# Spreading the output factors with VectorE's block transposes instead of a TensorE product

## The chip, the cores and the metric

The kernel runs on one core of a Trainium2 chip. The metric is the device time of one execution in microseconds. The core has five engines that run side by side and wait for each other through semaphores: TensorE (PE) multiplies matrices into PSUM, VectorE (DVE) and ScalarE (ACT) do elementwise work, GpSimd (POOL) does what is given to it of the same, SyncE (SP) issues most of the DMAs. Each engine runs its own instructions in the order in which the program gives them. ScalarE's queue can issue DMAs as well, and here it issues the few small ones at the start.

## The reference

Two stages follow each other. The first is causal attention with a decay in place of a softmax, over 8 batches, 8 heads, 576 positions and a head size of 64; the second is a feed-forward layer of 4608 tokens that takes the maximum of three products:

```python
scores = scale * np.matmul(q, k.transpose(0, 1, 3, 2))
gamma = 1.0 - 2.0 ** (-5.0 - np.arange(H, dtype=np.float32))
Dmat = np.where(rel >= 0, gamma[:, None, None] ** rel[None, :, :], 0.0)   # rel = query position - key position
x = np.matmul(scores * Dmat, v)            # then (B, H, S, D) -> (B*S, H*D)
h = np.maximum(np.maximum(x @ w1, x @ w2), x @ w3)
out = h @ w_out
```

The weights w1, w2, w3 and w_out come as 64-bit floats.

## The kernel before, in words

The tokens are cut into 36 chunks of 128 (`g`) and 9 tiles of 512 tokens (`t`). The decay gamma^(i-j) is split into a factor of the key, gamma^(-j), and one of the query, gamma^i / 8. The first is multiplied into v (`vd`, from `raws["v"]` and `gk`, line 273). The second, the output factor, is multiplied into the finished attention output when it goes from PSUM to SBUF (`xT`, line 224 through `output`, lines 550 to 559). It stands in `gq`, a tile of 128 partitions by 4 by 128: partition half c and index n belong to head 4c+n, the last axis is the position in the chunk, and all 64 partitions of a half hold the same numbers. A state carried from chunk to chunk (`state`, `keep`) brings in the older keys.

The order of all work is written out by hand: the framework's own ordering is off, and each engine gets its instructions in the order in which the Python code emits them. Lines 1060 to 1102 write the start, chunks 0 to 3. In that order:

- the memsets and the small DMAs: the rows of output factors (line 159) and the key factors `gk` (line 160), both on ScalarE's queue; ScalarE's table load and first copy follow (line 162);
- `warm(6)` (line 179), products of a tile of ones that only keep TensorE busy;
- `load(g)` (line 262): k, q and v of a chunk, 256 KB each, on SyncE's queue, with the first weights (`bits`, line 609) between them;
- `decay(0)`: vd of chunk 0, on GpSimd (line 273; also for chunks 1 and 2);
- `transposes(0)` (lines 298 and 299): TensorE transposes k (`kt`) and q (`qt`) of the chunk, ScalarE copies them out of PSUM as kT and qT;
- `scores(0)` (line 312), with VectorE's masks `st` (line 224 through `soon`), and `state(0)` (`kv`, line 425);
- `transposes(1)`, `decay(1)`;
- the product of the output factors (line 1082) and its copy from PSUM to `gq` (line 1083);
- `values(0)` (`o`, line 466), `keep(0)` (line 433), `scores(1)`, the factors multiplied into chunk 0's output (`xT`), `state(1)`, `transposes(2)`, `keep(1)`;
- `convert(2)`: the first two steps of turning 64-bit weights into 32-bit ones: `expo` (line 777) and `frac` (line 786) on VectorE with three operations of ScalarE (lines 779, 785 and 788); then `values(1)` and so on.

PSUM tiles come from pools with a fixed number of buffers that are handed out in turn. `ps_y` has two: the warming products, the product of the factors and the two `o` tiles of a chunk take turns in them. The second `o` tile of chunk 0 gets the buffer in which the factors were.

After the start the tiles of 512 tokens follow. In tile 0 the weights are converted by VectorE and ScalarE while TensorE does the plain products (`up`, line 934). From tile 1 on the feed-forward products are done by a scheme with fewer multiplications and more sums (line 909), with attention chunks between them.

How the factors reach `gq` before: two DMAs bring the 8 rows of 128 factors to two partitions, one for each half of the heads (`factors[0:2]`). `spreader[0:2, 1, :]` is a 2 by 128 matrix with ones where row c belongs to partition half c, made by a memset and two affine selects on GpSimd (lines 171 to 173). Their product is 128 partitions by 512, in one PSUM bank, with each factor row on all 64 partitions of its half; one copy takes it to `gq`.

Of the kernel before, what the change touches and what calls it, by code (L numbers as in the profile page):

```python
# [40 lines left out]
FP32 = mybir.dt.float32  # L41
# [4 lines left out]
ALU = mybir.AluOpType  # L46
PSUM = bass.MemoryType.PSUM

C = 128
# [49 lines left out]
def kernel(  # L99
# [14 lines left out]
    nc = tc.nc  # L114
    P = 128
    B, H, S, D = q.shape
    N, DM = out.shape
    DF = moe_w1.shape[1]
    NP = H // 2
# [12 lines left out]
    ppool = ctx.enter_context(tc.tile_pool(name="ppool", bufs=PARTS))  # L132
# [7 lines left out]
    ps_y = ctx.enter_context(tc.tile_pool(name="ps_y", bufs=2, space=PSUM))  # L140
# [4 lines left out]
    def half(j):  # L145
        return slice(D * j, D * (j + 1))
# [5 lines left out]
    const.tile([P, FILL // 4], FP32, name="fill")  # L152
    gq = const.tile([P, NP, C], FP32, name="gq")
    spreader = ppool.tile([P, NP, C], FP32, tag="part", name="spreader")
    for n in range(2):
        nc.vector.memset(spreader[:, n, :], 1.0)
    factors = ppool.tile([P, NP, C], FP32, tag="part", name="factors")
    for b in range(2):
        nc.scalar.dma_start(factors[0:2, b::2, :], out_decay[D * b].rearrange("(c u) x -> c u x", c=2))
    nc.scalar.dma_start(gk[:], key_decay)  # L160
    nc.vector.memset(one[:], 1.0)
    nc.scalar.copy(first[:], one[:])
# [4 lines left out]
    nc.gpsimd.memset(causal[:], 1.0)  # L167
    nc.gpsimd.affine_select(out=causal[:], in_=causal[:], compare_op=ALU.is_ge, fill=0.0,
                            base=0, channel_multiplier=-1, pattern=[[1, C]])

    for base, cm, step in ((0, -D, 1), (D - 1, D, -1)):
        nc.gpsimd.affine_select(out=spreader[0:2, 1, :], in_=spreader[0:2, 1, :], compare_op=ALU.is_ge, fill=0.0,
                                base=base, channel_multiplier=cm, pattern=[[step, P]])

    def warm(n):

        ps = ps_y.tile([P, P], FP32, tag="y", name="warm")
        for _ in range(n):
            nc.tensor.matmul(ps[:], lhsT=spreader[:, 0, :], rhs=spreader[:, 0, :], start=True, stop=True)
# [39 lines left out]
    def soon(step):  # L219

        if spread:
            urgent.append(step)
        else:
            step()
# [39 lines left out]
    def decay(g):  # L264
        factor = gk[:].unsqueeze(2).to_broadcast([C, H, D])
        t = raws.pop(("v", g))
        if spread or g >= CPT + 2:
            vds[g] = t
            scaling.extend(partial(nc.scalar.mul, t[:, h, :], t[:, h, :], gk[:, h:h + 1]) for h in range(H))
            return  # L270
        vds[g] = vpool.tile([C, H, D], FP32, tag="s", name="vd")
        engine = nc.gpsimd if g < CPT - 1 else nc.vector
        engine.tensor_tensor(vds[g][:], t[:], factor, op=ALU.mult)

    def pair(t, p):
        return t[:, 2 * p:2 * p + 2, :].rearrange("a h d -> a (h d)")

    def transposes(g, names="kq"):
        both = qks.setdefault(g, {})
        if both:  # L280
            pass
        elif g >= BY_CHUNKS:
            for n, tag in (("k", "kT"), ("q", "m1")):
                both[n] = att.tile([P, H, D], FP32, tag=tag, name=n + "T", bufs=2 if n == "k" else 3)
        else:
            both["k"] = att.tile([P, NP, C], FP32, tag="kT", name="kT", bufs=2)
            both["q"] = ppool.tile([P, NP, C], FP32, tag="part", name="qT")
        if g >= BY_PE:
            for n in ("k", "q"):
                soon(partial(nc.vector.transpose, both[n][:].rearrange("a p c -> a (p c)"),  # L290
                             raws.pop(("kx" if n == "k" else n, g))[:].rearrange("a x y i -> a (x y i)")))
            return
        for n in names:
            src = raws["k", g] if n == "k" else raws.pop(("q", g))
            pool, tag = (ps_r, "r") if g >= CPT else (ps_x, "x")
            pt = pool.tile([P, NP, C], FP32, tag=tag, name=n + "t")
            for p in range(NP):
                nc.tensor.transpose(pt[:, p, :], pair(src, p), ident[:C, :C])
            nc.scalar.copy(both[n][:], pt[:])
# [148 lines left out]
    def values(chunks, new_states=(), later=False, middle=()):  # L448

        def before(g):
            return C if start_of(g) is None else start_of(g)

        chore(len(urgent))
        t, i = divmod(chunks[0], CPT)
        if chunks[0] >= CPT:
            (chunk_values if chunks[0] >= BY_CHUNKS else parity_values)(chunks, t, i)
            return
        pool, tag = (ps_r, "r") if chunks[0] >= CPT - 1 else (ps_y, "y")  # L460
        o = [pool.tile([P, len(chunks), NP // 2, C], FP32, tag=tag, name="o") for _ in range(2)]
        for m, g in enumerate(chunks):
            for n in range(NP):
                for c in range(2):
                    h = head(c, n)
                    nc.tensor.matmul(o[n % 2][half(c), m, n // 2, :], lhsT=vds[g][:, h, :],
                                     rhs=sts[g, h % 2][:, h // 2, :], start=m == 0 and n < 2,
                                     stop=before(g) == 0, skip_group_check=True)
        for g in new_states:
            if g not in kvs:  # L470
                state(g)
        for step in middle:
            step()
        for m, g in enumerate(chunks):
            old = before(g)
            if old > 0:
                for n in range(NP):
                    for c in range(2):
                        h = head(c, n)
                        r = half(h % 2)  # L480
                        nc.tensor.matmul(o[n % 2][half(c), m, n // 2, :old], lhsT=states[g][r, h // 2, :],
                                         rhs=qks[g]["q"][r, h // 2, :old], start=False, stop=True,
                                         skip_group_check=True)
        finish = partial(output, chunks, o, t, i)
        if later:
            return finish
        finish()
# [582 lines left out]
    load_weights(2)  # L1070
    decay(0)

    transposes(0)
    warm(2)
    for j in range(2):
# [2 lines left out]
    state(0)  # L1078
    transposes(1)
    decay(1)  # L1080
    spread_factors = ps_y.tile([P, NP, C], FP32, tag="y", name="factors")
    nc.tensor.matmul(spread_factors[:], lhsT=spreader[0:2, 1, :], rhs=factors[0:2], start=True, stop=True)
    nc.vector.tensor_copy(gq[:], spread_factors[:])
    first_output = values([0], [0], later=True)
    keep(0)
    scores(1)
# [116 lines left out]
```

## Time and profile before

| | us |
|---|---|
| median of 3 runs (742.96 to 743.14) | 743.0 |
| the profiled execution, its own time | 742.99 |
| its span, first to last instruction | 740.9 |
| TensorE busy | 735.6 (99%) |
| VectorE busy | 575.2 (78%) |
| ScalarE busy | 344.7 (47%) |
| GpSimd busy | 37.2 (5%) |
| product of the factors, line 1082 (two records) | 0.59 and 0.69 |
| copy to `gq`, line 1083 | 0.69 |
| issue of the two factor DMAs on ScalarE's queue | 1.28 and 0.63 |

The profile is one execution. All times in it count from the first instruction. A matrix product of 32-bit floats shows as two records. L1082 is line 1082 of the kernel; operations that go through a helper are listed under the helper's line (224 for `soon`, 577 for sums), so that the names of the tiles tell them apart. An arrow in `vd<-vraw,gk` points from what is read to what is written. In lines with square brackets, the bracket holds the time that the engine stood idle before, and what ended it. Matmuls are pipelined, and a busy TensorE is not one at its peak.

### The profile page before, as it was taken

Reading aid. Unit: us, or ns where it says so; the run is one execution under the profiler, and the core shown is the slowest. Engines: PE = TensorE matmul, PEld = TensorE weight load, DVE = VectorE, ACT = ScalarE, POOL = GpSimd, SP = SyncE. Lnnn points to the kernel's source line nnn. Section 1 sums busy time; section 2 is a strip of 40 time slices with the busy share of each in tenths; the row PEclk is TensorE's granted clock in tenths of the full one; section 3 lists DMA queues with packets and bytes.
Section 4 is the critical chain, followed back from the end, with each engine's and each line's share of the span. In section 5 each row is a group of like instructions: output and inputs, shape, how many; then the busy total and the mean of one; then the engine's idle time right before and its main releaser. Section 6 shows DMA issues by size and latency. Waiting matters only on the chain.

```text
span 740.9 us, 17317 instructions
## 1 busy us (share of the span) xinstructions
PE 735.6 (99%) x6950; PEld 606.2 (82%) x6950; DVE 575.2 (78%) x1061; ACT 344.7 (47%) x731; POOL 37.2 (5%) x44
## 2 busy tenths in 40 slices
PE   8999999999999999999999999999999999999998
PEld 7644556888888888888888888888888888888887
DVE  4998898999886895699668876787768956893676
ACT  3664834554245434544354525543455255424441
POOL 3000000022000100000000000000100010000000
PEclk9999999999999999999999999999999999999999
DMA  9999432415142515141424243332514151000001
GB/s 216 241 252 258 100 74 79 93 18 99 62 85 42 100 33 105 38 83 47 108 52 73 44 98 75 60 57 56 116 22 95 38 106 31 1 31 29 0 1 57
DMA packets 226364, 58.82 MB, mean 79 GB/s; under 512 B 207588, under 2 KB 225004, under 8 KB 226284
## 3 DMA queue, kind: packets, MB, share of 16 engines
q1 hardware_dynamic: 225584, 57.71, 35.7%
q8 instruction: 54, 0.88, 0.5%
q14 instruction: 26, 0.21, 0.1%
q10 hardware_dynamic: 700, 0.01, 0.1%
HBM read 48.24 MB, written 9.44 MB: 78 GB/s over the span
## 4 chain that ended last, share of the span: by engine, by line
PE 98%; DVE 1%; DMA 1%; issue 0%; POOL 0%; SPq 0%; POOLq 0%
PE a L909 20%; PE b L909 17%; PE c L909 9%; PE up L934 8%; PE di L754 7%; PE d L909 6%; PE e L909 6%; PE dhc L754 5%; PE deg L754 3%; PE sk L380 3%; PE down L921 3%; PE o L530 2%; PE dfd L754 2%; PE o L537 2%; PE dx L661 1%; PE kv L383 1%
## 5 line engine op out<-in xcount | busy, mean ns | idle before, releaser
L897 DVE TENSOR_TENSOR part<-part 128x512 f32<-128x512 f32 x168 | 117.9, 702 | 86.5 <-ACT part L894 83.9
L894 ACT COPY part<-b 128x512 f32<-128x512 f32 x120 | 70.3, 586 | 163.5 <-PE b L909 161.5
L897 DVE TENSOR_TENSOR h<-h,part 128x512 f32<-128x512 f32 x120 | 83.3, 694 | 24.5 <-ACT h L894 20.5
L894 ACT COPY part<-a 128x512 f32<-128x512 f32 x96 | 56.3, 586 | 51.6 <-PE a L909 51.1
L212 ACT ACTIVATE vraw<-vraw,gk 128x64 f32<-128x64 f32 x240 | 76.8, 347 | 0.1
L909 PE MATMUL b<-s,n 128*128 128x256 f32 x288 | 73.9, 379 | 0.0
L934 PE MATMUL up<-xT,w 128*128 128x512 f32 (+2 forms) x160 | 64.2, 554 | 0.0
L909 PEld LDWEIGHTS b<-s,n 128*128 128x128 f32 x288 | 54.7, 190 | 7.4
L934 PEld LDWEIGHTS up<-xT,w 128*128 128x128 f32 x160 | 28.5, 190 | 29.4 <-issue 26.3
L909 PE MATMUL c<-xT,w 128*128 128x256 f32 x192 | 51.2, 389 | 0.0
L397 POOL TENSOR_TENSOR s<-s,gs_of 64x512 f32<-64x512 f32 x21 | 22.5, 1072 | 558.1 <-DVE s L395 441.7
L743 ACT COPY k<-di 128x256 f32<-128x256 f32 x49 | 18.2, 372 | 68.4 <-PE di L754 43.4
L909 PE MATMUL d<-s,w 128*128 128x256 f32 x192 | 49.8, 380 | 0.0
L909 PE MATMUL b<-xT,n 128*128 128x256 f32 x192 | 49.3, 379 | 0.0
L909 PE MATMUL a<-s,w 128*128 128x256 f32 x192 | 49.3, 379 | 0.0
L909 PE MATMUL a<-xT,w 128*128 128x256 f32 x192 | 49.3, 379 | 0.0
L909 PE MATMUL e<-xT,w 128*128 128x256 f32 x192 | 45.4, 379 | 0.0
L909 PE MATMUL a<-xT,n 128*128 128x256 f32 x192 | 45.4, 379 | 0.0
L909 PEld LDWEIGHTS e<-xT,w 128*128 128x128 f32 x192 | 36.5, 190 | 5.4 <-issue 0.5
L909 PEld LDWEIGHTS b<-xT,n 128*128 128x128 f32 x192 | 36.5, 190 | 5.0
L909 PEld LDWEIGHTS a<-xT,w 128*128 128x128 f32 x192 | 36.5, 190 | 5.0
L909 PEld LDWEIGHTS a<-s,w 128*128 128x128 f32 x192 | 36.5, 190 | 5.0
(201 smaller groups left out, 1382.7 us busy)
## 6 DMA issues: line engine op xcount, KB each, us to landing
bits<-in_moe_w_dram SPq DMA_DIRECT2D x36, 256.0 KB, 5.2
kraw<-in_k_dram SPq DMA_DIRECT2D x32, 256.0 KB, 3.1
vraw<-in_v_dram SPq DMA_DIRECT2D x32, 256.0 KB, 3.5
qraw<-in_q_dram SPq DMA_DIRECT2D x224, 32.0 KB, 2.1
kxraw<-in_k_dram SPq DMA_DIRECT2D x224, 32.0 KB, 2.0
out_dram<-osb SPq DMA_DIRECT2D x56, 128.0 KB, 1.7
bits<-in_moe_w_out_dram SPq DMA_DIRECT2D x6, 512.0 KB, 5.2
qraw<-in_q_dram SPq DMA_DIRECT2D x7, 256.0 KB, 4.9
```

The source lines that it names most:

```text
L212: scaling.popleft()()
L380: nc.tensor.matmul(s[half(c), h, :], lhsT=kT[half(c), h, :], rhs=qT[half(c), h, :], start=True, stop=True)
L397: nc.gpsimd.tensor_tensor(new, new, factor, op=ALU.mult)
L530: nc.tensor.matmul(o[m][half(c), n, u, :], lhsT=vds[g][half(m), h, :], rhs=sts[g][half(m), h, :], start=n == 0 and u == 0, stop=place(g, m ...
L537: nc.tensor.matmul(o[m][half(c), n, u, :], lhsT=stacks[g][half(m), h, :], rhs=qks[g]["q"][half(m), h, :], start=False, stop=True, skip_gro ...
L743: nc.scalar.copy(place, a)
L754: nc.tensor.matmul(banks[chain], lhsT=hidden(h, order, b, late_ones)[:, e], rhs=late["V"][v][:, e], start=begins and e == 0, stop=chain no ...
L894: nc.scalar.copy(of[step], ps[step[0]][:])
L897: nc.vector.tensor_tensor(of[dst], a, b, op=op)
L909: nc.tensor.matmul(ps[chain][:, e, :], lhsT=factor(w, 2 * fp + e), rhs=xS[t][x], start=n == 1 and e == 0, stop=ends, skip_group_check=True)
L921: nc.tensor.matmul(b[:], lhsT=h[:, fb, m * P:(m + 1) * P], rhs=w_sb["out", fb], start=fb == blocks[0], stop=fb == blocks[-1])
L934: nc.tensor.matmul(ps[:, a:b], lhsT=w_sb[i, fb][:, dc * P:(dc + 1) * P], rhs=xT[t][:, dc, a:b], start=dc == 0 and a == 0, stop=dc == NDC - ...
```

## The change

The factors no longer go through TensorE. Two DMAs (one for even, one for odd heads) now bring them as 128 rows of 32 numbers: row (n, i, j) holds positions 32j to 32j+31 of head pair i, eight times over (n), one row to a partition. VectorE transposes each of these 128 by 32 tiles in blocks of 32 by 32, which puts the position within a block of 32 on the partitions; four copies pick the columns of the heads that belong to a partition half and repeat each number 32 times along the row (`factors`, now 16 by 32 a partition); and one block transpose of 128 by 512 turns that into `gq`, the same contents as before. These seven instructions are emitted after `decay(0)` and before `transposes(0)`, so VectorE has them ahead of the masks of chunk 0. The second memset of `spreader`, the two affine selects, the product, its PSUM tile and the copy are gone; `rows` and `columns` lie in the free parts of `spreader`.

```diff
-    for n in range(2):
-        nc.vector.memset(spreader[:, n, :], 1.0)
-    factors = ppool.tile([P, NP, C], FP32, tag="part", name="factors")
+    nc.vector.memset(spreader[:, 0, :], 1.0)
+    factors = ppool.tile([P, 16, 32], FP32, tag="part", name="factors")
+    rows, columns = ([spreader[:, 1 + n, 32 * b:32 * b + 32] for b in range(2)] for n in range(2))
     for b in range(2):
-        nc.scalar.dma_start(factors[0:2, b::2, :], out_decay[D * b].rearrange("(c u) x -> c u x", c=2))
+        nc.scalar.dma_start(rows[b], out_decay[D * b:D * b + 8].rearrange("n u (j s) -> (n u j) s", s=32))
...
-    for base, cm, step in ((0, -D, 1), (D - 1, D, -1)):
-        nc.gpsimd.affine_select(out=spreader[0:2, 1, :], in_=spreader[0:2, 1, :], compare_op=ALU.is_ge, fill=0.0,
-                                base=base, channel_multiplier=cm, pattern=[[step, P]])
...
     decay(0)
 
+    for b in range(2):
+        nc.vector.transpose(columns[b], rows[b])
+        for c in range(2):
+            shape = [D, 2, 4, 32]
+            nc.vector.tensor_copy(
+                factors[half(c)].rearrange("p (u b j) s -> p u b j s", b=2, j=4)[:, :, b],
+                columns[b][half(c), 8 * c:8 * c + 8].rearrange("p (u j) -> p u j", j=4).unsqueeze(3).to_broadcast(shape))
+    nc.vector.transpose(gq[:].rearrange("p u x -> p (u x)"), factors[:].rearrange("p j s -> p (j s)"))
+
     transposes(0)
...
     decay(1)
-    spread_factors = ps_y.tile([P, NP, C], FP32, tag="y", name="factors")
-    nc.tensor.matmul(spread_factors[:], lhsT=spreader[0:2, 1, :], rhs=factors[0:2], start=True, stop=True)
-    nc.vector.tensor_copy(gq[:], spread_factors[:])
     first_output = values([0], [0], later=True)
```

## The prediction

> **What bounds the kernel now.** I read the chain of waits on the page first. It says that the time is TensorE's: what shortens the way to its first saturated stretch is worth its full length, what only relieves another engine is worth nothing.
>
> ```profile
> span 740.9 us, 17317 instructions
> PE 735.6 (99%) x6950; PEld 606.2 (82%) x6950; DVE 575.2 (78%) x1061; ACT 344.7 (47%) x731; POOL 37.2 (5%) x44
> PE 98%; DVE 1%; DMA 1%; issue 0%; POOL 0%; SPq 0%; POOLq 0%
> ```
>
> The change lies wholly before 11.5 us, so I read the same chain in order of time there (start, length, what).
>
> ```profile
> 6.59 1.05 POOL vd L273
> 7.65 0.04 issue
> 7.69 0.69 PE kv L425 x16
> 8.38 0.59 PE kt L298 x4
> 8.97 0.44 PE qt L298 x4
> 9.40 1.06 PE factors L1082 x2
> 10.47 0.02 issue
> 10.49 0.70 DVE gq L1083
> 11.19 0.04 issue
> 11.24 0.88 PE o L466 x12
> 12.11 1.09 PE s L312 x16
> ```
>
> The product of the factors and its copy stand on the chain. TensorE then waits for the copy: `o` takes two PSUM buffers of the pair that the factors used one of, so its second half can't begin before gq is copied out. From there the chain alternates between TensorE and VectorE up to 27.6 us, and by the windows TensorE is busy 94.50 of the 94.50 us from 27.5 to 122 and 615.86 of 618.90 after that. A shift at 27.6 us thus reaches the end.
>
> What can stop a shift before that is what TensorE and VectorE find missing when they come earlier. In the timeline (start, length, engine, line, operation):
>
> ```profile
> 15.06 1.04 POOL L273 TENSOR_TENSOR vd<-vraw,gk 128x512 f32<-128x512 f32 x1 [4.34 <-DMA vraw<-in_v_dram]
> 15.44 0.96 DVE L777 TENSOR_SCALAR expo<-bits 128x512 int32<-128x512 int32 x1
> 16.07 0.80 POOL L436 TENSOR_TENSOR state<-state,gs 128x256 f32<-128x256 f32 x1
> 16.31 0.83 DVE L786 TENSOR_SCALAR frac<-bits 128x512 int32<-128x512 int32 x1
> ```
>
> Both VectorE operations take 0.42 us elsewhere (22.83 and 23.16 us). Here each ends some 0.3 us after a GpSimd operation ends (16.10 and 16.87): they stood behind it. And the DMA engines are full: 1.07 of their capacity from 4 to 27.5 us.
>
> **What the skill says.** "SBUF — State Buffer", section "Who interferes with whom": copies and tensor-scalar operations of VectorE in a two-port mode and GpSimd's operations hold one port pair exclusively, the one that starts first for its whole length. The 0.96 and 0.83 us above agree. "VectorE: DVE Perf Modes", section "The three transpose paths": VectorE transposes 32x32 blocks only, which is why the change needs rows of 32 and transposes on both sides of a spreading copy. The trace's block transposes (0.70 us for 128x512) fit a plain pass over the elements; a transpose across blocks no run here shows. "DMA: Bandwidth & Descriptors", section "Issuing engines are not separate DMA queues": what ScalarE's queue issues runs on the same 16 engines as SyncE's loads; the next view agrees, since q10 (ScalarE's) takes its part while q1 fills the engines.
>
> ```profile
> q1 hardware_dynamic: 6330, 1.60, 100.7%
> q10 hardware_dynamic: 660, 0.01, 5.4%
> ```
>
> (From 2 to 9 us: packets, MB, share of 16 engines.)
>
> **Removed from the chain.** From 9.40 to 12.11 us, 2.71 us, stand the product (1.06), the copy (0.70), gaps (0.06) and the last 12 of the 16 matmul records of `o`. Without the product and without the PSUM wait `o` runs through: the same 16 take 1.21 us at 15.00. Saved: 2.71 - 1.21 = 1.50 us. What `o` needs besides is there: its masked scores (VectorE, 7.65 to 8.94), vd (7.63). The scores after it need qT, which ScalarE copies from 9.48 to 10.07, before they come at 10.6.
>
> **Removed off the chain, worth nothing.** One memset of 0.17 us (VectorE is idle until 7.65), two affine selects of 0.28 us on GpSimd (it then waits 3.66 us for v).
>
> **Added on VectorE**, ahead of the first masks: two transposes 128x32, four copies 64x256, one transpose 128x512. The last is in the trace: 0.70 us (STREAM_TRANSPOSE, kT). From tensor-tensor operations of 256 and 512 elements (0.415 and 0.685) I get 1.05 ns per element and 0.145 us fixed, so 128x32 costs an estimated 0.18 us. The copies are not shown: at one element a cycle 0.42 us each; at the two-port rate, as expo's 0.42 us for 512, 0.28. Sum: 0.36 + 1.1 to 1.7 + 0.70 = 2.2 to 2.7 us. I take 2.5. It is hidden in VectorE's idle time before 7.65 if the rows land in time. The first rows are issued at 0.80 and the second at about 2.1 (as before: 1.28 and 0.63 us of issue); gk, 128 runs as well, took 3.0 us to land. So they land at 3.8 and 5.1. After the second, 0.18 + 2 copies + 0.70 = 1.4 to 1.7 us remain: done at 6.5 to 6.8, 0.9 us before the masks want VectorE. With the cover gone there is slack behind it: the masks could start 0.8 us late before `o` at 9.6 misses them. The copies are over by 6.2, before GpSimd's vd at 6.6, so the port pair isn't contended there.
>
> **Added on the DMA engines.** 256 packets of 128 bytes for 8 of 512. A window in which nearly all packets are k and q blocks of 128 bytes (123 to 130 us: 3,716 packets, 47.4%) gives 14 ns each: 248 x 14 / 16 = 0.22 us of all engines. By bytes it is 28 KB at 230 GB/s = 0.12; at the whole run's mean of 18.8 ns, 0.29. I take 0.2. It delays what is queued behind: v of chunk 0 (landing 1.92 + 4.50 = 6.42), which frees vd and the chain from 6.59 on, and q of chunk 1 (3.90 + 4.7 = 8.6), on which qt at 8.7 waits. So it counts fully: +0.2 us. On ScalarE's queue the issues move by some tenths at most: its table load ends at 4.50 and its first copy of kT is wanted at 5.18.
>
> **What becomes late next.** With everything 1.3 us earlier, VectorE is done with chunk 0 at about 14.2 and turns to expo, whose weights were issued at 9.7 and took 4.9: 14.6, now 14.8. It waits there with xT and the masks of chunks 1 and 2 queued behind it. expo starts at 14.8, frac 0.33 later at 15.1, and GpSimd's vd of chunk 2 wants the port pair at 15.06 + 0.2 = 15.3. If VectorE is first by these 0.15 us, xT follows at 15.5, just when TensorE has its product (16.81 - 1.3): nothing lost. vd then ends at 16.6 and is needed at 17.2. k of chunk 3 lands at 10.95 + 4.9 + 0.2 = 16.1, wanted at 16.6. The rest shifts together.
>
> **Sum.** -1.50 + 0.20 = -1.3 us. The profiled execution took 742.99 us (span 740.9 and 2.1 around it), beside a median of 743.0: **741.7 us**.
>
> **Rivals.**
> 1. *GpSimd gets the port pair first.* For: 0.15 us of margin on estimates. If frac alone stands behind vd, it ends at 16.6 instead of 15.5, and the masks of chunk 2 start at 17.25 instead of 17.93 in the kernel before: 0.7 us gained, 742.3. If expo stands behind too, both end as they do now, and the DMA's 0.2 us is lost on top: 743.2.
> 2. *Slower: the rows land late.* The one mechanism is the queue at the DMA engines; VectorE runs in order, so the masks of chunk 0 wait behind it. For: the weights issued around 20 us took 9.4 us to land. Against: gk, on the same queue as the rows, took 3.0. Up to a landing at about 7.0 it costs nothing, from 8.3 it eats the gain, from 9.8 it shows as slower. At 2.1 + 9.3 = 11.4 the work ends at 13.0, 4.5 us after its deadline of 8.5: +4.5 - 1.3 gives 746.2.
> 3. *The packets hide.* If the added packets fall between the others, or the engine that ends v last was one of the two that carried the 512-byte rows, the 0.2 us isn't paid: 741.4.
> 4. *The product was hidden anyway*, because a load holds the chain behind it. Against: each landing that I could place comes before its use by 0.4 us or more, but for v of chunk 0 and q of chunk 1, which are counted, and the weights, which are rival 1.
>
> **Chances.** The forecast (741.5 to 742.0) 0.57, rival 1 with 4 (742.0 to 743.2) 0.20, rival 3 (below 741.5) 0.15, rival 2 0.08. The range 741.3 to 743.2 holds the first two and most of the third, and leaves out the late rows. A measurement of this kernel can tell about 0.2%, 1.5 us, from no change: 741.5 and 744.5. Faster: rival 3 and the low end of the forecast, 0.20. Slower: rival 2 from a landing at 9.8 on, 0.07. Same: 0.73.
>
> **What would show it.** Right: `o` of chunk 0 without a gap after qt at about 9.6, the scores at 10.8, the last transpose of VectorE over before 7, the first `up` stretch of TensorE (27.59) 1.3 us earlier. Wrong: masks of chunk 0 later than 8.5; v of chunk 0 landing well after 6.6; expo or frac stretched beyond 0.42 us at 15 us; a wait of TensorE between 11 and 27 us that is not there now; or a shift that is there at 27 us and gone at 122.

## The result and the profile after

The changed kernel takes 741.5 us (median of 18 executions, 740.89 to 743.42), the kernel before on the same chip 743.0 (18 executions, 742.62 to 743.41). The ratio is 0.9981, 95% interval 0.9974 to 0.9989: 1.5 us less by the medians. A difference of up to 0.2% counts as no change here, and the interval lies on both sides of that. The profiled execution took 741.6 us, and its page begins (span; busy time of the engines; then, from the chain that ended last, its shares by engine):

```profile
span 739.6 us, 17315 instructions
PE 734.1 (99%) x6948; PEld 605.8 (82%) x6948; DVE 576.1 (78%) x1066; ACT 345.0 (47%) x731; POOL 33.8 (5%) x42
...
PE 97%; SPq 1%; DMA 1%; DVE 0%; issue 0%
```

TensorE has two records less and 1.5 us less of work, GpSimd lost two operations, VectorE gained five and 0.9 us. SyncE's queue now has 1% of the chain, beside 1% of DMA as before. What they stand for is in the timeline of TensorE (start, length, engine, line, operation, number of records; in brackets the idle time before and what ended it):

```profile
9.10 1.09 PE L462 MATMUL o<-st,vd 128*64 128x128 f32 x16
10.12 1.16 PE L308 MATMUL s<-qT,kT 64*128 64x128 f32 x16
...
14.81 1.16 PE L308 MATMUL s<-qT,kT 64*128 64x128 f32 x16
16.67 0.63 PE L294 MATMUL kt<-ident,kraw 128*128 128x128 f32 x4 [0.70 <-DMA kraw<-in_k_dram]
...
21.19 2.85 PE L930 MATMUL up<-xT,w 128*128 128x384 f32 x8
```

The same places in the kernel before:

```profile
12.04 1.16 PE L312 MATMUL s<-qT,kT 64*128 64x128 f32 x16
...
16.73 1.16 PE L312 MATMUL s<-qT,kT 64*128 64x128 f32 x16
17.83 0.66 PE L298 MATMUL kt<-ident,kraw 128*128 128x128 f32 x4
...
22.50 2.85 PE L934 MATMUL up<-xT,w 128*128 128x384 f32 x8
```

And the first long `up` stretch on the chain (start, length, what), before:

```profile
27.59 15.11 PE up L934 x48
```

and after:

```profile
26.28 15.10 PE up L930 x48
```

`o` of chunk 0 now runs through, without product or gap. The scores of chunk 1 come at 10.12 instead of 12.04: 1.92 us earlier. The whole 1.92 is still there at the scores of chunk 2 (16.73 before, 14.81 now). Then TensorE stands 0.70 us at the k of chunk 3, and of the 1.92 us 1.16 are left (17.83 to 16.67); at `up` it is 1.31 (22.50 to 21.19). The long `up` stretch of the chain also begins 1.31 earlier, and the span ends 1.3 earlier. In the stretch from 27.5 to 122 us TensorE is again busy for 94.50 of 94.50 us.

VectorE's timeline of the same execution:

```profile
3.60 0.21 DVE L1070 STREAM_TRANSPOSE spreader<-spreader 128x32 f32<-128x32 f32 x1 [2.50 <-DMA spreader<-in_out_decay_dram]
3.84 0.59 DVE L1073 COPY factors<-spreader 64x256 f32<-64x256 f32 x2
4.68 0.21 DVE L1070 STREAM_TRANSPOSE spreader<-spreader 128x32 f32<-128x32 f32 x1 [0.25 <-DMA spreader<-in_out_decay_dram]
...
5.55 0.71 DVE L1076 STREAM_TRANSPOSE gq<-factors 128x512 f32<-128x512 f32 x1
7.63 1.29 DVE L220 TENSOR_TENSOR st<-s,causal 128x512 f32<-128x512 f32 x2 [1.37 <-PE s L308]
...
15.29 0.43 DVE L773 TENSOR_SCALAR expo<-bits 128x512 int32<-128x512 int32 x1 [1.70 <-DMA bits<-in_moe_w_dram]
15.63 0.42 DVE L782 TENSOR_SCALAR frac<-bits 128x512 int32<-128x512 int32 x1
```

The seven added operations take 2.3 us and are over at 6.26; the masks then wait 1.37 us for TensorE, not for VectorE. The port pair that the forecast worried about does no harm: expo and frac have their plain 0.42 us. This time GpSimd comes second, at 15.76, and takes 1.19 us instead of 1.04:

```profile
6.09 1.04 POOL L269 TENSOR_TENSOR vd<-vraw,gk 128x512 f32<-128x512 f32 x1 [3.62 <-DMA vraw<-in_v_dram]
15.76 1.19 POOL L269 TENSOR_TENSOR vd<-vraw,gk 128x512 f32<-128x512 f32 x1 [5.64 <-DMA vraw<-in_v_dram]
```

The DMA queues from 2 to 9 us (packets, MB, share of 16 engines) show the added packets in q10, which had 660 there before:

```profile
q1 hardware_dynamic: 6514, 1.64, 103.7%
q10 hardware_dynamic: 937, 0.04, 8.4%
```

Over the whole run q10 has 976 packets instead of 700, so 276 were added and not the forecast's 248: besides the 256 rows of 128 bytes in place of 8 of 512, there are 28 packets of 4 bytes more.

### The profile page after: what moved, and what is told of

Its sections match the earlier page's. It is cut to its first block, busy times and chain, and to the rows that moved or that the text cites. A ratio compares the mean times of both kernels' runs of the same rounds, so it can differ in the third digit from the quotient of the medians.

```text
span 739.6 us, 17315 instructions
## 1 busy us (share of the span) xinstructions
PE 734.1 (99%) x6948; PEld 605.8 (82%) x6948; DVE 576.1 (78%) x1066; ACT 345.0 (47%) x731; POOL 33.8 (5%) x42
## 4 chain that ended last, share of the span: by engine, by line
PE 97%; SPq 1%; DMA 1%; DVE 0%; issue 0%
PE a L905 20%; PE b L905 17%; PE c L905 9%; PE up L930 8%; PE di L750 7%; PE d L905 6%; PE e L905 6%; PE dhc L750 5%; PE deg L750 3%; PE sk L376 3%; PE down L917 3%; PE o L526 2%; PE dfd L750 2%; PE o L533 2%; PE dx L657 1%; SPq L258 1%
```

## Experiments

The theory to test: the gain is that of the product's place on the chain and of the PSUM buffer that it shares with `o`; what was added is hidden; what limits the gain is the load that comes late next, k of chunk 3. Rivals: the gain comes from something else that the change moves (DMA order, VectorE), or the additions cost a part of it. Times below are medians, each beside the kernel before on its own chip (743.0 to 743.1).

**Only the product's place.** The kernel before, with its product kept and issued earlier, in the place of two warming products:

```diff
     transposes(0)
-    warm(2)
+    spread_factors = ps_y.tile([P, NP, C], FP32, tag="y", name="factors")
+    nc.tensor.matmul(spread_factors[:], lhsT=spreader[0:2, 1, :], rhs=factors[0:2], start=True, stop=True)
+    nc.vector.tensor_copy(gq[:], spread_factors[:])
...
     decay(1)
-    spread_factors = ...   (the same three lines)
```

> The kernel before with the TensorE product of the factors and its copy moved ahead, into the place of the two warming products after the first transposes. My theory: what the change gained is the place on the chain, not the engine; the product then runs at 5.5 us where TensorE waits for qT, and `o` of chunk 0 runs without a gap. Gain 1.3 to 1.6 us against the kernel before, 741.4 to 741.7. Rival (the gain of the changed kernel comes from its lighter two-row loads and from VectorE doing the spreading): under half of it, 742.3 or more.

Measured: 742.1 us, ratio 0.9997 (0.9986 to 1.0008), but in no single heap: of 14 executions six took 741.1 to 741.6, three 742.1 to 742.3, and five 743.3 to 745.2. The profile is of one that took 741.17. Its chain (start, length, what):

```profile
5.72 1.05 PE factors L1075 x2
...
9.50 1.02 PE o L466 x16
10.52 1.09 PE s L312 x16
```

The product is on the chain and costs its full 1.05 us, in the place of 0.6 us of warming products, and still the execution is as short as the changed kernel's: `o` runs through in 1.02 us, and at k of chunk 3 there is no wait (`up` follows at 26.00). In these six executions the gain is there with the product kept, with the old loads of the factors and with nothing added on VectorE, so it comes from the product's place. By its median the kernel missed the expected 741.4 to 741.7. What the long executions lose was not in any theory; it is taken up at the end of this section.

**Only the PSUM buffer.** The product stays where it was, but takes its tile from another pool, so `o` needn't wait for the copy:

```diff
-    spread_factors = ps_y.tile([P, NP, C], FP32, tag="y", name="factors")
+    spread_factors = ps_r.tile([P, NP, C], FP32, tag="r", name="factors")
```

> The kernel before, product in its old place, but its PSUM tile from the other pool, so that `o` doesn't wait for the copy to gq. It splits the 1.50 us: the wait goes (0.44 us), the product's 1.06 stays. My theory: 742.5, 0.3 to 0.6 faster than before. Rival (the PSUM wait was nearly all of it): 741.6.

Measured: 742.4 us (13 executions), ratio 0.9992 (0.9984 to 1.0000), 0.6 less than before. The chain:

```profile
9.45 1.05 PE factors L1082 x2
10.50 1.02 PE o L466 x16
11.53 1.09 PE s L312 x16
```

From product to scores 2.08 us pass instead of 2.71: 0.63 of the stretch was the wait for the copy, 1.05 the product. Together they are 1.68, which is what the changed kernel saves there (below).

**None of the additions.** The changed kernel without the rows and without their spreading; `gq` is set to ones, so the decay of the query is missing in the output:

```diff
-        nc.scalar.dma_start(rows[b], out_decay[D * b:D * b + 8].rearrange("n u (j s) -> (n u j) s", s=32))
...
-    (the two transposes, four copies and the last transpose)
+    nc.vector.memset(gq[:], 1.0)
```

> The changed kernel without the factors: no rows are loaded, nothing is spread, gq is filled with ones by one memset, so the output lacks the query's decay. It prices all that the change added (256 packets and seven operations of VectorE). My theory: the additions are hidden but for the packets, so 0 to 0.3 us faster than the changed kernel, 741.2 to 741.5. Rival (the spreading costs time on VectorE): 1 us or more faster, 740.5.

Measured: 741.4 us (15 executions), ratio 0.9979 (0.9971 to 0.9986), which is 0.1 below the changed kernel and within its interval. So the additions, VectorE's 2.3 us and the packets together, cost about 0.1 by the medians. The executions of the two kernels (741.05 to 742.23 here, 740.89 to 743.42 there) overlap too far to tell 0.1 from nothing or from the forecast's 0.2; a cost of 1 us, the rival's, is excluded. The profiled execution was its longest (742.23) and shows that the loads scatter without them too: v of chunk 0 lets GpSimd start at 6.77, later than in the changed kernel (6.09), and TensorE waits 1.10 us for k of chunk 3.

**Twice the additions.** The seven operations of VectorE once more behind the first seven:

```diff
     nc.vector.transpose(gq[:].rearrange("p u x -> p (u x)"), factors[:].rearrange("p j s -> p (j s)"))
+    (the same loop and transpose again)
```

> The changed kernel with the seven operations of the spreading done twice, so that VectorE is done at about 8.7 instead of 6.3 us and the masks of chunk 0 are a good 1 us late. My theory: `o` of chunk 0 starts some 0.7 us late, but TensorE stands 0.70 us at k of chunk 3 in the changed kernel, and the delay is swallowed there: 741.5 to 741.8, no later at the first product of the weights than 26.5. Rival (nothing behind it absorbs): 0.7 to 0.9 us slower than the changed kernel, 742.3.

Measured: 742.4 us (13 executions), ratio 0.9993 (0.9985 to 1.0001), 0.9 more than the changed kernel: here my theory fell and the rival was right. The chain:

```profile
8.47 0.04 DVE gq L1084
...
9.11 1.26 DVE st L220 x2
...
10.41 0.88 PE o L462 x12
11.29 1.09 PE s L308 x16
```

The masks come at 9.11 instead of 7.63, and the spreading is now on the chain. The scores are about 1.1 later than in the changed kernel, so the 1.5 us met only about 0.4 of slack. (Some 0.46 us of both delays is not the spreading's: in this execution TensorE begins the scores of chunk 0 at 6.83 instead of 6.37. Their difference, the slack, stays.) The theory had it that the wait for k of chunk 3 would take this up. In the profile it does in part (that wait is gone, and `up` comes at 26.77 instead of 26.28), but the median pays the full 0.9. Of that profile's 1.1 us of longer span 0.5 is there at 27 us, and it is still 0.5 at TensorE's last product (end at 737.0 instead of 736.5). The other 0.6 lies behind VectorE's last operation, when only the last store is under way: from there to the end of the span it is 3.26 us here, 2.62 in the changed kernel, and 2.62 to 2.75 in all other profiles. Whether the other executions of this kernel have the long store too is not shown, so the 0.9 of the median is not fully placed.

**k of chunk 3 earlier.** The changed kernel with this load issued ahead of the first weights:

```diff
+    load(CPT - 1, "k")
...
-    load(CPT - 1, "kq")
+    load(CPT - 1, "q")
```

> The changed kernel with k of chunk 3 loaded ahead of the first weights instead of behind v of chunk 2. Theory C (the start is held by the loads as a whole: what comes earlier pushes something else back that is wanted just then): the stall of TensorE at k of chunk 3 goes, the first weights and v of chunk 2 land 1 us later, expo with the masks of chunk 2 behind it starts at 16 or later: 741.6 to 742.4, no better than the changed kernel. Theory D (only k of chunk 3 is late): the 0.7 us come back, 740.8.

Measured: 742.9 us (13 executions), ratio 0.9999 (0.9991 to 1.0007): 1.4 more than the changed kernel, nearly the whole gain, and worse than even theory C's 741.6 to 742.4. From the timeline:

```profile
16.15 0.66 PE L294 MATMUL kt<-ident,kraw 128*128 128x128 f32 x4
...
16.91 1.21 POOL L269 TENSOR_TENSOR vd<-vraw,gk 128x512 f32<-128x512 f32 x1 [6.43 <-DMA vraw<-in_v_dram]
...
18.17 0.69 PE L421 MATMUL kv<-vd,kraw 128*64 128x64 f32 x16 [1.37 <-POOL vd L269]
```

The wait for k is gone. The weights and v of chunk 2, now behind it, land some 1.2 us later instead (expo at 16.45, vd at 16.91), and TensorE waits 1.37 us for vd. The chain itself runs over the late weights: expo, frac, xT and the masks of chunk 2, which let `o` go on at 19.13. Moving this load ahead in the full queue moved the wait.

**One load less.** The changed kernel without the load of v of chunk 2; its vd is made from v of chunk 1, so v of chunk 2 is missing in the output:

```diff
-    load(2, "v")
+    raws["v", 2] = raws["v", 1]
```

> The changed kernel without the load of v of chunk 2: vd of that chunk is made from v of chunk 1, so the output is that of another v there. One load of 256 KB is gone between the first weights and k of chunk 3, which then lands 1 us earlier. Theory C (the loads bound the start after the change): TensorE no longer stops before the transpose of k of chunk 3, and 0.4 to 0.8 us come out: 740.7 to 741.1. Rival (the loads are hidden, the stall belonged to single executions): 741.4 to 741.6, as the changed kernel.

Measured: 741.2 us (13 executions), ratio 0.9977 (0.9968 to 0.9985): 0.2 to 0.3 below the changed kernel, less than the 0.4 to 0.8 expected and more than the rival's nothing, with intervals that overlap. TensorE finds k of chunk 3 at 16.12 without a wait, and `up` comes at 25.88. So by the medians this load holds back some 0.3 us, not the 0.6 that the one profile shows.

**The changed kernel again**, for a second profile:

> The changed kernel once more, beside the others, for a second profile of it. Time as before, 741.5. Theory C/D: where TensorE stops before the transpose of k of chunk 3 differs between executions with the landing of that load (15.1 to 17.4 us in the profiles so far), by up to 0.8 us; if it always stands there by 0.7 us, the stall belongs to the kernel and not to the execution.

Measured: 741.6 us (11 executions), ratio 0.9978 (0.9970 to 0.9987). Its profile has the wait for k of chunk 3 again:

```profile
17.01 0.63 PE L294 MATMUL kt<-ident,kraw 128*128 128x128 f32 x4 [0.42 <-DMA kraw<-in_k_dram]
```

The long `up` stretch comes at 26.57, only 1.02 us earlier than before, although the wait is shorter than in the first profile. Here TensorE itself was late: `o` of chunk 0 begins at 9.71 instead of 9.10. At the start one record of a product of 128 columns takes 0.42 us, later 0.27; that step comes at about 4.9 us in the first profile of the changed kernel and at about 7.0 in this one.

**The warming products.** Two runs for what the first experiment's long executions are made of: the early product with the warming products kept behind it, and the changed kernel without `warm(2)`.

```diff
     nc.vector.tensor_copy(gq[:], spread_factors[:])
+    warm(2)
```

> As the product moved ahead (the earlier run), but with the two warming products kept behind it. Five of that kernel's 14 times lay 2 to 4 us above the rest. Theory A (the product uses two rows of the array only, and in the place of the warming products it lets TensorE's clock stay low for one more window in some executions): with the warming products the high times are gone, and the scores of chunk 0 come 0.6 us later, so 741.6 to 742.2 with a spread under 1 us. Theory B (the spread has another cause, such as where the loads land): the high times stay, a third of the executions at 743 or more.

Measured: 741.9 us, ratio 0.9991 (0.9981 to 1.0001); twelve of 14 executions at 741.6 to 742.5, two at 745.5 and 746.0. With the products kept the long executions are not gone, against theory A, and not a third, against theory B; two of 14 and five of 14 are too few to say that they are rarer.

```diff
     transposes(0)
-    warm(2)
```

> The changed kernel without the two warming products after the first transposes. Theory A: they keep the clock, so some executions come out 2 to 4 us higher, as with the product in their place. Theory B: nothing happens, TensorE only waits there for qT: 741.3 to 741.7, as the changed kernel.

Measured: 741.8 us, ratio 0.9986 (0.9980 to 0.9992); six of 21 executions at 742.7 to 743.3. Of the changed kernel's 29 executions one is that long. So the warming products do something, but theory A's 2 to 4 us were not seen; the profile is of a short execution (741.19) and doesn't show what the long ones lose.

**The early product, three single executions**, to have a long one in a profile:

> A second look at the kernel with the product moved ahead, to meet one of its executions at 743 or more (5 of 14). Theory A (clock): in such a one the matmuls of 128 columns still take 0.42 us after 6 us, where the others take 0.27 to 0.31 from 5.3 on. Theory B (loads): the matmuls are as fast as in the profile at 741.2, and TensorE waits for a load.

> A third look at the same kernel, with the same two expectations.

> A fourth look at the same kernel, with the same two expectations.

Measured: 741.88, 744.87 and 741.55 us. TensorE's timeline in the long execution:

```profile
7.75 2.08 PE L312 MATMUL s<-qT,kT 64*128 64x128 f32 x16
...
14.07 1.16 PE L312 MATMUL s<-qT,kT 64*128 64x128 f32 x16
```

and in the short one of 741.55 us:

```profile
6.59 1.16 PE L312 MATMUL s<-qT,kT 64*128 64x128 f32 x16
```

The same 16 products take 2.08 us in one and 1.16 in the other (the product of the factors before them 2.07 and 1.12), and in the long execution TensorE's work takes 1.6 to 1.9 times as long until some 13 us. The scores of chunk 1 are then 3.7 us late (14.07 to 10.35), and the execution is 3.3 us longer; no load is waited for. For this execution theory A is right: TensorE's rate, not a load. The two short ones wait for k of chunk 3 as the changed kernel does, 1.02 us (741.88) and 0.67 us (741.55).

That fits the Trainium skill, "TensorE: Matmul & The Clock Gate", section "Part 1: The HAM clock gate (the "warmup" mystery)": TensorE starts at half its clock and is let up to the full one after a window of some 3.4 us with enough work, a window that doesn't begin with the kernel. The traces agree in that every profile has one such step, from 0.42 to 0.27 us a record, and that it comes at different times: between 4.4 and 7.1 us in all the others, at about 13.4 us in the long one. By that figure of the skill it is late by two windows, an estimate (13.4 less 6.8 is 6.6, back among the others). That the product with only two rows keeps a window from counting as busy is argued from the skill's page and from the two warming runs, and it doesn't explain two windows, since the product lasts 2.07 us. So the cause of the late step is open, and so is whether the other long executions have it too.

## Why the prediction was right, and where its terms were not

The forecast was 741.7 us, a range of 741.3 to 743.2, and no change of over 0.2% as the likeliest. The median is 741.5, 0.19% less than before, on the border between the forecast (from 741.5 on) and rival 3 (below it). The sum of -1.3 us is what the two profiles differ by, both at the first `up` of the chain and in the span. Its terms are not: they are off in both directions and make up for each other. The second profile of the changed kernel has -1.0 at the same place, so the agreement to a tenth is also luck.

- **Removed from the chain: -1.50 forecast, -1.69 measured.** Product, wait and `o` took 2.71 us before; `o` alone takes 1.02. The 1.21 that stood for it was taken from an `o` that starts with a wait for xT. The mechanism is as written: the other PSUM buffer alone brings 0.63, the product's 1.05 the rest.
- **Packets: +0.20 forecast, not seen.** The step "so it counts fully" failed. In the profile v of chunk 0 let GpSimd start at 6.09 rather than 6.59, and the chain came to `o` 0.23 earlier, not 0.2 later. It isn't that the packets speed v up: over all profiles this start lies between 6.04 and 6.77, and the latest is that of the kernel without the rows. The 0.2 drowns in a scatter that one profile doesn't show, and the kernel without the additions leaves about 0.1 for all of them. That fits rival 3, but doesn't exclude the 0.2. The second reason for the term, that `qt` of chunk 1 waits for q, isn't in the trace before: `qt` follows `kt` there at 8.80 without a wait.
- **Added on VectorE: 2.2 to 2.7 us forecast, 2.3 measured.** The copies took 0.285 to 0.291 us each, the rate of expo that gave the lower end. Rows landed for VectorE at 3.6 and 4.7 (3.8 and 5.1 forecast); all is over at 6.26 (6.5 to 6.8). It is hidden, as said. The slack behind it, 0.8 us forecast, is nearer to 0.4 by the doubled spreading. Rival 2 needed landings some 5 us later and was not seen.
- **The port pair (rival 1): it did not happen.** VectorE was first: frac started 0.13 us before vd (0.15 forecast), though both 0.5 us later than forecast, since weights and v both landed later. What the Trainium skill says in "SBUF — State Buffer", section "Who interferes with whom", that the later of the two waits, shows on the other side: vd took 1.19 us instead of 1.04. With so small a margin this owes something to luck. In two other kernels GpSimd was first: expo and frac took 0.96 and 0.83 us with the doubled spreading, 0.78 and 0.84 with the early product and the warming products, and TensorE had no wait for it before 27 us, so the rival's price was not seen there either.
- **What becomes late next: the step "k of chunk 3 lands ... 16.1, wanted at 16.6" failed.** It took 5.71 us to land instead of 4.9, and with 1.92 us gained TensorE was there at 15.97. With the wait of 0.70 us, 1.31 of the 1.92 are left at `up`. This is rival 4's thought, a load that holds the chain, which I had excluded because each landing of the one profile had 0.4 us of room. By the run with one load less it costs 0.2 to 0.3 us on average.
- **A shift at 27 us reaches the end: right.** From the chain's first `up` to the end of the span it is 713.3 us before and in the changed kernel, and 713.1 to 713.4 in all other profiles but for the 713.9 with the doubled spreading, where the 0.6 more lie behind TensorE's last product.

In the profile: -1.69 from the chain, -0.23 from v's landing, +0.61 at k of chunk 3, together -1.31. Had I counted the removal in full and the packets at nothing, I would have forecast -1.7 and 741.3; the landing of k takes the difference. So the total owes something to luck; the mechanism of the removal does not, for the early product and the other PSUM buffer show it. Open stay why the same load takes 4.9 us in one execution and 5.7 or 6.1 in the next, and why the last store takes 0.6 us longer in the profile with the doubled spreading.

## What to carry to other kernels

A small product between two stages can cost its length plus the wait of whoever shares its PSUM buffers (1.05 and 0.63 us here): look for both on the chain, for the second went away with another pool alone. After a gain, list the loads by the room that they have before their use in the new order, and take their scatter from several executions; k of chunk 3, to which one profile seemed to leave 0.5 us of room, came 0.7 us late in the next, and pulling it forward in the full queue made others late. Compare several profiles of the start before you trust a tenth of a us: TensorE's step to its full rate alone moved `o` of chunk 0 by 0.6 us between two executions of one kernel. Work that is hidden stays free only as long as its cover: doubling it cost 0.9 us here.

## What the runs showed of the hardware

- With one product of 2 rows and 512 columns in TensorE's first 8 us, in the place of warming products, six of 17 executions were some 2 to 4 us longer. In the one of them that was profiled TensorE kept its low rate until some 13 us (scores 2.08 us instead of 1.16). The profile page's row of the granted clock reads 9 throughout in that execution too; the low rate shows only in the lengths.
- Copies of VectorE that met GpSimd's vd took longer: with the doubled spreading, two copies in a row that take 0.59 us elsewhere took 1.00 from 6.59 on, while vd ran from 6.10 to 7.14.
- The same 256 KB load (k of chunk 3), issued at 10.8 to 11.5 us, took 4.9 us to land in the kernel before, 5.71 and 6.06 in two profiles of the changed kernel, and 5.80 in the one without rows: the scatter of the landings is larger than any difference that 276 packets more or less make here.
